# Pooled keys turned three at a time, scores of a head in two matmuls: pooled attention and a max-of-three feed-forward on one core

## The chip, the cores and the metric

The kernel runs on one core of a Trainium2 chip. The metric is the device time of one execution in microseconds (us), as the median of several runs. TensorE is the matrix engine (PE in the profile, PEld its weight loads), DVE is VectorE, ACT is ScalarE, POOL is GpSimd, SP the engine that issues many of the DMAs.

## The reference

Eight batches of attention with 8 heads, 576 positions and 64 elements per head. Keys and values are averaged over groups of 8 positions first, so each head has 576 queries and only 72 keys. The result, 4608 rows of 512, goes through a feed-forward layer whose hidden activation is the maximum of three products.

```
k_p = k.reshape(B, H, 72, 8, 64).mean(axis=3)
v_p = v.reshape(B, H, 72, 8, 64).mean(axis=3)
scores = scale * (q @ k_p.T);  attn = softmax(scores)
x = (attn @ v_p), heads side by side          # 4608 x 512
h = max(x @ w1, x @ w2, x @ w3)               # 4608 x 768
out = h @ w_out                               # 4608 x 512, float32
```

## The kernel before

The whole program is unrolled, and the order of instructions on each engine is the order in which the code issues them; a framework adds the semaphores. Tokens of the feed-forward are taken in nine blocks of 512. `block(n, plan, parts)` walks through the parts of block n (the hidden products at line 345, evacuated by ScalarE at line 351 and VectorE at line 353, and the output products at lines 390 and 394), and between two parts (a slot) it inserts the attention steps that `plan` names for that slot. Attention of batch n + 1 runs in this way between the matmuls of the feed-forward of block n. The last blocks (function `weave`) use the order written out in `ORDER`, with other products (lines 669 and 732).

The attention of a batch has these steps:

- GpSimd adds up groups of eight keys (`fold_k`, lines 150 to 153); for batch 1 VectorE does it, and batch 0 has a path of its own (`sum_k0`, `put_k0`). The sum `kp` has 96 partitions of 6 pooled keys each, 64 elements per key, in bfloat16.
- `k`: `turn_k` turns the keys so that the 64 elements lie on partitions. `keys` does it with six transposes on TensorE, one for each of the six keys of a partition, into one PSUM tile `pkt`. Two copies (`fill_kz`, line 193) take it to `kz`.
- `kz` holds the keys of all heads twice: once on partitions 0 to 63 with zeros below (parity 0) and once on partitions 64 to 127 with zeros above (parity 1). The reason is the layout of the queries: `qT` has nine groups of 64 queries per head, and two neighbouring groups lie above each other on the 128 partitions. A score matmul contracts over all 128 partitions and picks its half by the zeros. There are two `kz` buffers, for even and odd batches. For batches 1 and 2 both copies are on VectorE, for later ones parity 0 is copied by VectorE and parity 1 by ScalarE.
- `q`: the queries are turned by TensorE (`turn_q`) or, from batch 3, by a transposing DMA (`T`).
- `s0` to `s7`: `scores` of one head. Five groups of 64 queries belong to parity 0 and four to parity 1. They are written as 320 columns, then 192 and 64: the code splits where a PSUM bank ends, at column 512. Then `exp` on ScalarE, 72 partitions by 576.
- `v`, `x`: the weighted values, their division by the sum of the weights, and the turn of the result for the feed-forward.

In `plan`, for batches 3 to 5, `k` stands in slot 0 and the first scores in slot 2. For batch 2 (`plan1`) `k` is in slot 6 and the first score in slot 11; for batch 1 in slots 24 and 26 of block 0. Batch 6 is turned in slot 17 of block 4, batch 7 at the start of `ORDER` (scored flat, over 512 columns at a time). Batch 0 is scored by `scores4` and `scores2`.

In the middle of the program, the PSUM tag `att` holds two buffers of two banks (`pkt`, `psc`, `pav`), `pw` three of one bank, and `tr` one.

Of the kernel before, what the change touches and what calls it, by code (L numbers as in the profile page):

```python
# [14 lines left out]
def kernel(  # L15
# [11 lines left out]
    nc = tc.nc  # L27
    dt = mybir.dt
    F32, BF16, F16 = dt.float32, dt.bfloat16, dt.float16

    B, H, S, D = q.shape
    POOL = 8
    Sp = S // POOL
# [17 lines left out]
    const = ctx.enter_context(tc.tile_pool(name="const", bufs=1))  # L51
# [10 lines left out]
    def psum(shape, dtype, name, tag, bufs):  # L62
        return pools[-1].tile(shape, dtype, name=name, tag=tag, bufs=bufs)

    kts, vts, qbs, kps, qTs, ets = {}, {}, {}, {}, {}, {}
# [50 lines left out]
    ident = const.tile([128, 128], BF16, name="ident", tag="ident")  # L116
# [6 lines left out]
    for sign in (1, -1):  # L123
        nc.gpsimd.affine_select(
            out=pick, in_=pick, compare_op=ALU.is_ge, fill=0.0, base=7 * (sign < 0),
            pattern=[[sign, 6], [-8 * sign, 128]], channel_multiplier=6 * sign)
    for i in range(3):
        load_w(slice(256 * i, 256 * i + 256))
    nc.gpsimd.dma_start(
        out=wo_sb, in_=moe_w_out.rearrange("(jc p) c -> p jc c", p=128))  # L130
# [5 lines left out]
    load_v(2, nc.gpsimd)  # L136


    kz_all = [const.tile([128, 2, H, 128], BF16, name=f"kz{i}", tag=f"kz{i}")
              for i in range(2)]  # L140
    nc.vector.memset(kz_all[0], 0.0)
    vp_all = const.tile([Sp, B, H, 65], F16, name="vp", tag="vp")
    nc.vector.memset(vp_all[:, :, :, D:65], float(POOL))
    xT = const.tile([128, KCH, TOK], F16, name="xT", tag="xT")
# [13 lines left out]
    def fold_k(b, e, i0=0, i1=6):  # L158
        if b not in kps:
            new_kp(b)  # L160
        fold(e, kts[b][:, i0:i1], kps[b][:, i0:i1], F16 if e is nc.vector else F32)
# [12 lines left out]
    def turn_q(b, n0, n1, evac, tag):  # L174
        if b not in qTs:
            qTs[b] = sb2.tile([128, 2 * NG, 128], BF16, name="qT", tag="qT")
        pqt = psum([128, n1 - n0, 128], BF16, name="pqt", tag=tag[0],
                       bufs=tag[1])
        qf = qbs[b].rearrange("p hp t d -> p (hp t d)")
        for n in range(n0, n1):  # L180
            nc.tensor.transpose(pqt[:, n - n0, :], qf[:, 128 * n:128 * n + 128],
                                ident)
        evac(out=qTs[b][:, n0:n1, :], in_=pqt)  # L183

    def keys(b, tag):
        pkt = psum([D, 6, 96], BF16, name="pkt", tag=tag[0], bufs=tag[1])
        for i in range(6):
            nc.tensor.transpose(pkt[:, i, :], kps[b][:, i, :], ident[0:96, 0:96])  # L188
        return pkt

    def fill_kz(b, par, h0, h1, pkt, evac):
        rows = slice(64 * par, 64 * par + 64)
        evac(out=kz_all[b % 2][rows, par, h0:h1, 0:Sp].rearrange(
                 "p h (r i) -> p h r i", i=6),
             in_=pkt[:, :, 12 * h0:12 * h1].rearrange("p i (h r) -> p h r i", r=12))

    def turn_k(b):
        pkt = keys(b, ATT if len(pools) < 3 else SC)
        for par, evac in enumerate((nc.vector.tensor_copy, nc.scalar.copy)):
            fill_kz(b, par, 0, H, pkt, evac if b > 2 else nc.vector.tensor_copy)  # L200

    def score(b, h, out, tp, i0, i1):

        f = NG * (h // 2) + tp
        n = f // 2
        nc.tensor.matmul(out, kz_all[b % 2][:, f % 2, h, :],  # L206
                         qTs[b][:, n + i0:n + i1, 64 * (h % 2):64 * (h % 2) + 64],
                         start=True, stop=True)

    def exp(out, in_):  # L210
        nc.scalar.activation(out=out, in_=in_, func=FT.Exp, scale=1.0 / 64.0)  # L211

    def new_et(b):
        ets[b] = sb2.tile([Sp, H, S], F16, name="et", tag="et")

    def scores(b, h):
        psc = psum([128, 1024], F32, name="psc", tag="att", bufs=2)
        score(b, h, psc[:, 0:320], 0, 0, 5)
        score(b, h, psc[:, 320:512], 1, 0, 3)
        score(b, h, psc[:, 512:576], 1, 3, 4)  # L220
        exp(ets[b][:, h, :], psc[0:Sp, 0:S])

    def scores_flat(b, j):

# [11 lines left out]
    def turn_x(b, c0, keep, xn, tag, evac=nc.scalar.copy):  # L236
        if b > 2:
            g0 = S * b + c0
            nc.sync.dma_start_transpose(
                out=xT[:, :, g0 + keep:g0 + 128],  # L240
                in_=xn.rearrange("p g h d -> p (g h d)")[keep:128])
            return
        pxt = psum([128, KCH, 128], F16, name="pxt", tag=tag[0], bufs=tag[1])
        for kc in range(KCH):
            nc.tensor.transpose(  # L245
                pxt[:, kc, :],
                xn[:, kc // 2, 2 * (kc % 2):2 * (kc % 2) + 2, :], identh)
        g0 = S * b + c0
        evac(out=xT[:, :, g0 + keep:g0 + 128], in_=pxt[:, :, keep:128])  # L249

    def values(b, c0):
        tag = (ATT0, ATT, ("val", 1))[len(pools) - 1]
        pav = psum([128, 2, 512], F32, name="pav", tag=tag[0], bufs=tag[1])
        for h in range(H):
            nc.tensor.matmul(  # L255
                pav[:, h // 4, 65 * (h % 4):65 * (h % 4) + 65],
                ets[b][:, h, c0:c0 + 128], vp_all[:, b, h, :],
                start=True, stop=True)
        pv = pav[:, :, 0:260].rearrange("p g (h e) -> p g h e", e=65)
        rcp = sb3.tile([128, 2, 4], F32, name="rcp", tag="rcp")  # L260
        nc.vector.reciprocal(out=rcp, in_=pv[:, :, :, 64])  # L261
        xn = sb3.tile([128, 2, 4, D], F16, name="xn", tag="xn", bufs=6)
        nc.vector.tensor_tensor(  # L263
            out=xn, in0=pv[:, :, :, 0:D],
            in1=rcp.to_broadcast([128, 2, 4, D]), op=ALU.mult)
        return xn
# [11 lines left out]
    def do(b, steps):  # L278

        for name in steps.split():
            i = int(name[1:] or 0)
            if name[0] in "qQ":
                turn_q(b, *QS[i], nc.vector.tensor_copy if name[0] == "Q"
                       else nc.scalar.copy, TR)
            elif name[0] == "T":
                qTs[b] = sb2.tile([128, 2 * NG, 128], BF16, name="qT", tag="qT")
                nc.sync.dma_start_transpose(
                    out=qTs[b], in_=qbs[b].rearrange("p hp t d -> p (hp t d)"))  # L290
            elif name[0] == "k":
                turn_k(b)
            elif name[0] == "K":
                fold_k(b, nc.vector)
            elif name[0] == "s":
                if i == 0:
                    new_et(b)
                (scores if len(pools) < 3 else scores_flat)(b, i)
            elif name[0] == "d":
                sub_w(i)  # L300
            elif name[0] == "z":
                nc.vector.memset(kz_all[1], 0.0)
            elif name[0] == "w":
                turn_w(i, nc.scalar.copy if i % 2 else nc.vector.tensor_copy)
            elif name[0] == "v":
                xns[b, i] = values(b, CHUNKS[i][0])
            else:
                turn_x(b, *CHUNKS[i], xns[b, i], TR if b == 1 else ATT,
                       nc.vector.tensor_copy if name[0] == "X" else nc.scalar.copy)
# [4 lines left out]
    def sub_w(i, j0=0, j1=2, wi=(1, 2)):  # L314

        part = slice(256 * i + 128 * j0, 256 * i + 128 * j1)
        for t in [w_sb[w] for w in wi]:
            nc.vector.tensor_tensor(out=t[:, :, part], in0=t[:, :, part],  # L318
                                    in1=w_sb[0][:, :, part], op=ALU.subtract)

    def turn_w(jc, evac):
        pwt = psum([128, KCH, 128], F16, name="pwt", tag=TR[0], bufs=TR[1])
        for kc in range(KCH):
            nc.tensor.transpose(pwt[:, kc, :], w_sb[0][:, kc, bass.ts(jc, 128)], identh)
        evac(out=w1T[:, jc, :], in_=pwt.rearrange("p k c -> p (k c)"))
# [103 lines left out]

    def put_k0(a, par, evac):  # L430
        i = 3 * min(a, 1)
        evac(out=kz_all[0][64 * par:64 * par + 64, par, :, 0:Sp].rearrange(
                 "p h (r i) -> p h r i", i=6)[:, :, :, i:i + 3],
             in_=pk0[a].rearrange("p i (h r) -> p h r i", r=12))

# [23 lines left out]
    for par in range(2):  # L459
        put_k0(0, par, nc.scalar.copy)  # L460
# [36 lines left out]
    def block(n, plan, parts, folds=()):  # L497

        for slot, _ in enumerate(part for stage in parts for part in stage(n)):
            if slot == 0 and n > 0:  # L500
                pool_work(n, mms[-1])
            for b, steps in plan.get(slot, ()):
                if b < B:
                    do(b, steps)
            if folds and slot in FOLDS:
                next(folds.pop(0))
# [335 lines left out]
```

## Time and profile before

| | us |
|---|---|
| median of 5 runs (231.42 to 232.32) | 231.8 |
| the profiled execution | 231.8 |
| its span, first to last instruction | 230.1 |
| TensorE busy | 221.0 |
| GpSimd busy | 139.7 |
| VectorE busy | 128.6 |
| ScalarE busy | 121.1 |
| 42 transposes of keys, mean of one | 0.210 |
| 9 copies of keys on VectorE, mean of one | 0.749 |
| 5 copies of keys on ScalarE, mean of one | 0.630 |

The duration of a matmul in the profile includes its way through the array, so successive matmuls overlap: what a matmul costs the stream is the distance from its start to the next start. A group line has the line of the code, engine, operation, what is written and read, shapes and count, then the busy time in us and the mean of one in ns, then the idle time of the engine before it and what ended it. In a timeline the columns are start, length, engine, line, operation.

### The profile page before, as it was taken

To read this page: it belongs to the slowest core of one execution; us is meant where nothing else is said; L and a number is where in the kernel's file an instruction comes from. 1 tells how busy PE (TensorE), PEld (TensorE's weight loads), DVE (VectorE), ACT (ScalarE), POOL (GpSimd) and SP (SyncE) were. 2 spreads that over 40 slices of the span, in tenths; PEclk is the share of its full clock that TensorE was granted. 3 is DMA by queue.
4 is the path that set the end of the run, shared out by engine and by line. 5 is a ranking of instruction groups with operands and counts; after the bars stand their busy time and mean duration, and the time that the engine had idled before them with its cause. 6 is when DMAs were issued, how large, how long until landed. Compare 5 with 4: busy or idle time off the path is not lost.

```text
span 230.1 us, 4529 instructions
## 1 busy us (share of the span) xinstructions
PE 221.0 (96%) x1756; PEld 136.4 (59%) x1756; DVE 128.6 (56%) x235; ACT 121.1 (53%) x216; POOL 139.7 (61%) x115
## 2 busy tenths in 40 slices
PE   7788999999999999999999999999999999999991
PEld 2467645568655555545554555555777666786781
DVE  3668875048326333622462246279578877897720
ACT  2277425755864575247524852683786446464330
POOL 7974302999849999999999739900343433910010
PEclk9999999999999999999999999999999999999998
DMA  6999999999469999987998599961331535302336
GB/s 179 206 196 196 212 203 211 186 188 229 71 115 204 226 159 218 171 188 131 212 175 192 85 226 184 181 134 30 86 68 38 113 68 88 86 0 48 91 70 162
DMA packets 47157, 33.53 MB, mean 146 GB/s; under 512 B 27104, under 2 KB 41888, under 8 KB 47136
## 3 DMA queue, kind: packets, MB, share of 16 engines
q0 software_dynamic: 16944, 16.98, 45.8%
q1 hardware_dynamic: 30032, 16.13, 32.8%
q8 instruction: 14, 0.23, 0.4%
q10 hardware_dynamic: 160, 0.13, 0.3%
q14 instruction: 7, 0.06, 0.1%
HBM read 34.60 MB, written 9.44 MB: 191 GB/s over the span
## 4 chain that ended last, share of the span: by engine, by line
PE 89%; DMA 4%; DVE 2%; POOL 1%; issue 1%; ACT 1%; POOLq 0%; DVEq 0%
PE pw L345 27%; PE po L394 18%; PE po L390 12%; PE pA L732 7%; PE psc L206 5%; PE pav L255 4%; DMA vt<-in_v_dram 4%; PE pC L732 3%; PE pm L332 2%; PE oA L669 2%; PE pB L732 2%; PE pxt L245 1%; PE pkt L188 1%; DVE xn L263 1%; PE oC L669 1%
## 5 line engine op out<-in xcount | busy, mean ns | idle before, releaser
L345 PE MATMUL pw<-xT,mw 128*128 128x512 f16 (+1 forms) x336 | 73.1, 349 | 0.3 <-ACT xT L249 0.2
L394 PE MATMUL po<-mwo,hT 128*128 128x512 f16 (+1 forms) x198 | 46.8, 372 | 0.0
L353 DVE TENSOR_TENSOR hT<-t,pw 128x512 f16<-128x512 f16 (+1 forms) x42 | 25.5, 610 | 36.8 <-ACT et L211 25.1
L399 ACT COPY osb<-po 128x512 f32<-128x512 f32 (+1 forms) x32 | 18.5, 579 | 42.2 <-PE po L394 42.2
L345 PEld LDWEIGHTS <-mw 128*128 128x128 f16 x336 | 28.9, 98 | 19.7 <-DVE mw L318 0.6
L211 ACT ACTIVATE et<-psc 72x576 f16<-72x576 f32 (+2 forms) x54 | 35.2, 660 | 6.5 <-PE psc L206 6.3
L150 POOL TENSOR_TENSOR half<-vt 72x2048 f32<-72x2048 f16 x7 | 28.4, 4059 | 12.8 <-DMA vt<-in_v_dram 12.4
L390 PE MATMUL po<-wm,xT 128*128 128x512 f16 (+1 forms) x132 | 33.0, 373 | 0.0
L351 ACT ACTIVATE t<-pw 128x512 f16<-128x512 f32 (+1 forms) x42 | 22.5, 537 | 14.7 <-PE pw L345 13.0
L263 DVE TENSOR_TENSOR xn<-pav,rcp 128x512 f16<-128x512 f32 x40 | 27.7, 691 | 1.4
L394 PEld LDWEIGHTS <-hT 128*128 128x128 f16 x198 | 18.3, 97 | 16.2
L151 POOL TENSOR_TENSOR half<-half 72x1024 f32<-72x1024 f32 (+1 forms) x13 | 27.2, 2095 | 1.0
L206 PEld LDWEIGHTS <-kz 128*128 128x128 bf16 x191 | 17.6, 98 | 14.4 <-ACT qT L183 1.1
L206 PE MATMUL psc<-qT,kz 128*128 128x320 bf16 (+2 forms) x168 | 22.4, 246 | 0.8 <-DVE qT L183 0.6
L150 POOL TENSOR_TENSOR half<-ktFalse 96x1536 f32<-96x1536 f16 x6 | 18.6, 3095 | 5.3 <-DMA ktFalse<-in_k_dram 5.1
L255 PEld LDWEIGHTS <-et 72*128 72x128 f16 x320 | 15.4, 98 | 7.7 <-issue 0.4
L738 ACT CAST pad<-pA 128x512 f16<-128x512 f32 x27 | 15.3, 587 | 8.5 <-PE pA L732 6.0
L261 DVE RECIPROCAL rcp<-pav 128x8 f32<-128x8 f32 x40 | 8.2, 206 | 18.3 <-PE pav L255 18.1
L390 PEld LDWEIGHTS <-xT 128*128 128x128 f16 x132 | 11.9, 98 | 9.0
L255 PE MATMUL pav<-vp,et 72*128 72x65 f16 x320 | 16.9, 194 | 0.1
L713 DVE SCALAR_TENSOR_TENSOR hT<-pad 128x512 f16<-128x512 f16 x18 | 14.4, 810 | 1.8 <-ACT pad L742 1.4
L732 PEld LDWEIGHTS <-sw 128*128 128x128 f16 x144 | 13.7, 98 | 2.7
(106 smaller groups left out, 276.2 us busy)
## 6 DMA issues: line engine op xcount, KB each, us to landing
out_dram<-osb SPq DMA_DIRECT2D x62, 128.0 KB, 3.1
ktFalse<-in_k_dram POOLq DMA_DIRECT2D x7, 576.0 KB, 7.2
qb<-in_q_dram POOLq DMA_DIRECT2D x7, 576.0 KB, 13.5
vt<-in_v_dram POOLq DMA_DIRECT2D x7, 576.0 KB, 11.5
mw<-in_moe_w_dram POOLq DMA_DIRECT2D x9, 256.0 KB, 9.6
ktTrue<-in_k_dram SPq DMA_DIRECT2D x3, 384.0 KB, 5.2
mwo<-in_moe_w_out_dram POOLq DMA_DIRECT2D x1, 768.0 KB, 13.7
qb<-in_q_dram POOLq DMA_DIRECT2D x2, 288.0 KB, 7.9
```

Source lines behind the costliest of these rows:

```text
L150: e.tensor_tensor(out=f, in0=t[:, :, 0:4, :], in1=t[:, :, 4:8, :], op=ALU.add)
L151: e.tensor_tensor(out=f[:, :, 0:2, :], in0=f[:, :, 0:2, :], in1=f[:, :, 2:4, :], op=ALU.add)
L206: nc.tensor.matmul(out, kz_all[b % 2][:, f % 2, h, :], qTs[b][:, n + i0:n + i1, 64 * (h % 2):64 * (h % 2) + 64], start=True, stop=True)
L211: nc.scalar.activation(out=out, in_=in_, func=FT.Exp, scale=1.0 / 64.0)
L255: nc.tensor.matmul(pav[:, h // 4, 65 * (h % 4):65 * (h % 4) + 65], ets[b][:, h, c0:c0 + 128], vp_all[:, b, h, :], start=True, stop=True)
L263: nc.vector.tensor_tensor(out=xn, in0=pv[:, :, :, 0:D], in1=rcp.to_broadcast([128, 2, 4, D]), op=ALU.mult)
L345: mm = nc.tensor.matmul(pw, w_sb[wi][:, kc, bass.ts(jc, 128)], xT[:, kc, col], start=(kc == 0), stop=(kc == KCH - 1))
L351: nc.scalar.activation(out=t, in_=pw, func=FT.Relu)
L353: nc.vector.tensor_tensor(out=hT[:, jc, c0:c1], in0=t, in1=pw, op=ALU.max)
L390: nc.tensor.matmul(po, xT[:, kc, bass.ts(m, 128)], wm_sb[:, kc, c], start=(kc == 0), stop=False)
L394: nc.tensor.matmul(po, hT[:, jc, bass.ts(mm, 128)], wo_sb[:, jc, c], start=False, stop=(jc == JCH - 1))
L732: mm = nc.tensor.matmul(p[:, w], a[:, kc, bass.ts(g, 128)], b[:, kc, :], start=(i in FIRST and w + kc == 0), stop=(w + kc == 2), skip_grou ...
```

## The change

The keys of a batch are turned by three transposes in place of six. Each takes two of the six keys of a partition together, 128 columns, so that in `pkt` the even keys are on partitions 0 to 63 and the odd ones on 64 to 127. Each parity of `kz` is then filled by two copies, one for the even and one for the odd keys, each writing every second element of 72; four copies in all, on the same engines as before. `kz` becomes two tiles for each buffer, one per parity, and its two memsets become four of half the size. In `scores`, the 576 columns start at column 192 of the two banks, so that the border falls between the 320 columns of parity 0 and the 256 of parity 1, and two matmuls do.

```
-    kz_all = [const.tile([128, 2, H, 128], BF16, name=f"kz{i}", tag=f"kz{i}")
-              for i in range(2)]
-    nc.vector.memset(kz_all[0], 0.0)
+    kz_all = [[const.tile([128, H, 128], BF16, name=f"kz{i}{par}", tag=f"kz{i}{par}")
+               for par in range(2)] for i in range(2)]
+    for par in range(2):
+        nc.vector.memset(kz_all[0][par], 0.0)
...
     def keys(b, tag):
-        pkt = psum([D, 6, 96], BF16, name="pkt", tag=tag[0], bufs=tag[1])
-        for i in range(6):
-            nc.tensor.transpose(pkt[:, i, :], kps[b][:, i, :], ident[0:96, 0:96])
+        pkt = psum([128, 3, 96], BF16, name="pkt", tag=tag[0], bufs=tag[1])
+        for i in range(3):
+            nc.tensor.transpose(pkt[:, i, :],
+                                kps[b][:, 2 * i:2 * i + 2, :].rearrange("p i d -> p (i d)"),
+                                ident[0:96, 0:96])
         return pkt
-
-    def fill_kz(b, par, h0, h1, pkt, evac):
-        rows = slice(64 * par, 64 * par + 64)
-        evac(out=kz_all[b % 2][rows, par, h0:h1, 0:Sp].rearrange(
-                 "p h (r i) -> p h r i", i=6),
-             in_=pkt[:, :, 12 * h0:12 * h1].rearrange("p i (h r) -> p h r i", r=12))

     def turn_k(b):
         pkt = keys(b, ATT if len(pools) < 3 else SC)
         for par, evac in enumerate((nc.vector.tensor_copy, nc.scalar.copy)):
-            fill_kz(b, par, 0, H, pkt, evac if b > 2 else nc.vector.tensor_copy)
+            for odd in range(2):
+                (evac if b > 2 else nc.vector.tensor_copy)(
+                    out=kz_all[b % 2][par][64 * par:64 * par + 64, :, 0:Sp].rearrange(
+                         "p h (r i t) -> p h r i t", i=3, t=2)[:, :, :, :, odd],
+                     in_=pkt[64 * odd:64 * odd + 64].rearrange("p i (h r) -> p h r i", r=12))
...
-        nc.tensor.matmul(out, kz_all[b % 2][:, f % 2, h, :],
+        nc.tensor.matmul(out, kz_all[b % 2][f % 2][:, h, :],
...
     def scores(b, h):
         psc = psum([128, 1024], F32, name="psc", tag="att", bufs=2)
-        score(b, h, psc[:, 0:320], 0, 0, 5)
-        score(b, h, psc[:, 320:512], 1, 0, 3)
-        score(b, h, psc[:, 512:576], 1, 3, 4)
-        exp(ets[b][:, h, :], psc[0:Sp, 0:S])
+        score(b, h, psc[:, 192:512], 0, 0, 5)
+        score(b, h, psc[:, 512:768], 1, 0, 4)
+        exp(ets[b][:, h, :], psc[0:Sp, 192:768])
...
-                nc.vector.memset(kz_all[1], 0.0)
+                for par in range(2):
+                    nc.vector.memset(kz_all[1][par], 0.0)
...
-        evac(out=kz_all[0][64 * par:64 * par + 64, par, :, 0:Sp].rearrange(
+        evac(out=kz_all[0][par][64 * par:64 * par + 64, :, 0:Sp].rearrange(
```

## The prediction

> **What bounds the kernel now.** I read the page first (busy shares and the chain), then the timeline around one turn of the keys, then the groups by shape, then the tile view of `pkt`. On the page, TensorE is busy nearly all the time, the chain runs through it, and its clock is granted in full.
>
> ```profile
> PE 221.0 (96%) x1756; PEld 136.4 (59%) x1756; DVE 128.6 (56%) x235; ACT 121.1 (53%) x216; POOL 139.7 (61%) x115
> ...
> PEclk9999999999999999999999999999999999999998
> ...
> PE 89%; DMA 4%; DVE 2%; POOL 1%; issue 1%; ACT 1%; POOLq 0%; DVEq 0%
> ```
>
> From about 52 us to the end of its work at 225 us TensorE waits for almost nothing, so what its instruction stream sheds there comes off the time, unless a late copy puts a wait in its place. "Busy" hides small holes, so I look at start times. Timeline of TensorE alone, around the keys of batch 3 (start, length, operation):
>
> ```profile
> 78.44 0.38 PE L345 MATMUL pw<-xT,mw 128*128 128x512 f16 x1
> 78.75 0.44 PE L188 MATMUL pkt<-ident,kp 96*64 96x96 bf16 x6
> 79.12 0.39 PE L345 MATMUL pw<-xT,mw 128*128 128x512 f16 x1
> ```
>
> A 512-column matmul is followed by the next after 0.216 us in this trace (8 starts fill 1.73 us of the chain). Here 0.31 us pass before the first transpose: 0.096 of them are empty. Six transposes at 0.042 need 0.255; 0.375 pass. So a turn occupies 0.68 - 0.216 = 0.467 us, plus 0.011 by which the following matmul is late (0.227 instead of 0.216): 0.48. The same holes of 0.096 and 0.098 stand before and after each of the seven turns (37.1, 55.7, 78.7, 101.5, 124.3, 144.0, 159.5 us).
>
> **Part 1, three transposes with 128 weight columns.** The holes are found where the weights are 96x64. The value pooling has 96 rows and 128 columns:
>
> ```profile
> 13.37 0.81 PE L170 MATMUL pvp<-vt,pick 96*128 96x256 f16 x6
> 14.02 0.44 PE L206 MATMUL psc<-qT,kz 128*128 128x64 bf16 x4
> ```
>
> Six of 256 columns take 0.65 us to the next start, 0.109 each, the same as 256 columns elsewhere: no hole. I therefore cost the new turn (96x128) at 3 x 0.042 = 0.127 us and nothing around it. Saved: 0.48 - 0.127 = 0.355 us a turn, times 7 = 2.49 us. If 64 columns were not the cause and both holes stayed, only 3 x 0.042 = 0.127 a turn, 0.89 in all, would be saved.
>
> **Part 2, two score matmuls.** It drops one matmul in each of 8 heads of batches 1 to 6 (batch 7 is scored flat, batch 0 otherwise): 48. In the stream of starts near 105 us the three are 0.136, 0.083 and 0.028 apart; 256 columns elsewhere cost 0.109, so 0.111 becomes 0.109: 2 ns each, 0.1 us in all. The Trainium skill ("TensorEngine Tiling (Array Packing)", Instruction Overhead) gives every matmul about 60 cycles of overhead, which at this trace's 2.4 columns per ns would be 25 ns each, 1.2 us in all. The row decides: 64 columns at 28 ns are paid by columns, and the weight loads lie under the running matmul. Exp reads 576 columns over two banks as before: nothing.
>
> **Part 3, the copies.** Each 64x576 copy becomes two of 64x288 with every second element written. The nearest rows are batch 0's own 64x288 fills:
>
> ```profile
> L193 DVE COPY kz<-pkt 64x576 bf16<-64x576 bf16 x9 | 6.7, 749 | 12.5 <-PE pkt L188 12.4
> ...
> L193 ACT COPY kz<-pkt 64x576 bf16<-64x576 bf16 x5 | 3.2, 630 | 4.3 <-DVE kz L193 4.3
> ...
> L432 ACT CAST kz<-pk 64x288 bf16<-64x288 f32 x2 | 1.0, 476 | 4.1 <-PE pk L427 4.1
> ...
> L432 DVE CAST kz<-pk 64x288 bf16<-64x288 f32 x2 | 0.9, 473 | 0.7 <-PE pk L427 0.6
> ```
>
> They start 0.505 apart on both engines. Bounds: below, ACT's rows of 256 and 512 columns (372 and 585) put 288 at 398, and DVE's 749 for 576 at one column per 1.04 ns puts it at 449; above, no cheaper than before (749 and 630) if every second element costs like two. I take 473 and 476, as shape and type of the output agree.
>
> Times below are in the frame of the trace, as if nothing earlier had moved.
>
> *Batch 1 (all four on DVE).* The copies start at 37.36 (before 37.61, less the hole and three transposes, 0.25). The fourth ends at 37.36 + 3 x 0.505 + 0.473 = 39.35, and the second score matmul, which needs its weights, can start about 0.09 later (a weight load is 98 ns), 39.44. Before, it started at 39.44; unhindered it would now be there at 39.09. The 0.355 are lost, and nothing gives them back: the next hole, 0.29 at 46.2, is a wait for an exp that TensorE's own scores feed.
>
> *Batch 2 (four on DVE).* Queued behind them is the max of line 353:
>
> ```profile
> 56.15 1.51 DVE L193 COPY kz<-pkt 64x576 bf16<-64x576 bf16 x2 [0.54 <-PE pkt L188]
> 57.70 0.75 DVE L353 TENSOR_TENSOR hT<-t,pw 128x256 f16<-128x256 f16 x2
> ```
>
> It now starts at 55.905 + 4 x 0.505 = 57.93 instead of 57.70; it signals 0.43 after its start (57.70 to 58.13 before), so at 58.36, and the `pw` group that takes its buffer, at 58.44 before and 58.08 if unhindered, starts at 58.40: 0.04 of the 0.355 remains.
>
> *Batches 3 to 7 (two on DVE, two on ScalarE).* The tile view of `pkt` says what ScalarE's copy waits for:
>
> ```profile
> its engine sat idle before it (us, times) until:
>   PE pkt L188: 12.4, 6
>   DVE kz L193: 4.3, 5
> ```
>
> It waits for DVE's copy, though by their semaphores the first score weight loads wait for one of the two copies each (even parity for DVE, odd for ScalarE). So it isn't the tile `kz` that binds them but the read of one `pkt`, and splitting `kz` by parity takes no wait away. The Trainium skill ("PSUM — Partial Sum Buffer", PSUM bank collisions raise a hardware error) has the reason: two engines must not read one bank in the same 32 partitions at once, while other partitions of that bank are free. `pkt` is one bank, and the new copies read 64 partitions each. Kept by partitions, ScalarE's first copy waits for DVE's first, its second for DVE's second. Kept by whole banks, both wait for DVE's second. No row of the trace tells which; this is the largest unknown, so I work out both for batch 3.
>
> By partitions: DVE 78.98 to 79.45 and 79.48 to 79.96; ScalarE (free at 79.45) 79.49 to 79.96 and 79.99 to 80.47. The weight load for odd parity is now due at 80.86 - 0.355 = 80.51: in time. By banks: ScalarE 79.99 to 80.97, the score at about 81.07 where it was 80.995: the whole 0.355 is gone and 0.07 besides.
>
> Batch 6 has 1.5 us of slack (its keys are turned at 144.0, scored at 147.4): 0.355 in both. Batch 7: DVE is late there (copy at 160.60), so by partitions ScalarE ends at 162.09, `osb` behind it (162.28 before) frees its bank in time, 0.355 remains; by banks it ends at 162.6 and nothing remains.
>
> **Part 4, the split memsets** (lines 141 and 302, 0.91 us each): about 0.1 us more on DVE, while it waits for the first keys and at 30 us, where TensorE has no hole. Nothing.
>
> **The sum**, against the profiled execution (231.8 us, span 230.1, the rest of 1.7 unchanged; it equals the median of the runs). By partitions: batch 1 0, batch 2 0.04, batches 3 to 7 5 x 0.355 = 1.78, scores 0.1: 1.9, so **229.9 us**.
>
> **Rivals.** *A: whole banks.* 0 + 0.04 - 3 x 0.07 + 0.355 + 0 + 0.1 = 0.3 saved, 231.5; with copies at the lower bounds batches 3 to 5 give some 0.05 each and the sum is 0.8, 231.0. For it: a bank is the simplest unit to guard. Against it: nothing in this trace. *B (slower): the writes of every second element cost like full ones.* Copies of 750 (0.781 apart) and 630: batch 1's second score at 40.53 (1.09 late), batch 2's `pw` group at 59.51 (1.07 late), batches 3 to 5 0.27 late each, batch 7 0.22 late, batch 6 and the scores give 0.46 back: 2.7 us, 234.5. It decides once the copies exceed about 0.58 us, where 0.11 more per copy has eaten 1.9. Against it: batch 0's fills write runs of three and are only 23 (DVE) and 78 ns (ScalarE) over contiguous. *C: the holes stay.* Then the copies start 0.127 earlier, not 0.25; batch 1 ends 0.12 and batch 2 0.08 later than before, five turns give 0.127 each, the scores 0.1: 0.5 saved, 231.3. Against it: the 96x128 row.
>
> **How the numbers follow.** Main case 0.46 (own range 229.3 to 230.6, from copies at their lower bound to 40 ns longer), A 0.36, B 0.12, C 0.06. Range: 229.3 to 231.8 takes in A and C and leaves B and the ends out. This kernel's runs tell apart 0.3%, 0.7 us. Faster than that: nearly all of the main case and a third of A, 0.57. Within: most of A, C, 0.30. Slower: B and the tail of A, 0.13.
>
> **What would show it.** Right: `pkt` in 21 transposes of 96*128 with no hole around them, two score matmuls a head, ScalarE's first fill starting about 0.5 us after DVE's first. Wrong: ScalarE's first fill 1 us after it (A); fills above 0.58 us (B); 0.1 us before and after the new turn (C); or a wait of a `pw` or score matmul that I didn't foresee behind the longer DVE queue.

## The result and the profile after

The changed kernel takes 230.86 us (median of 29 runs, 230.47 to 232.13) beside 231.55 us for the kernel before (50 runs). The ratio is 0.9968, with a 95% interval of 0.9960 to 0.9976: faster by 0.3%, about 0.74 us. The forecast was 1.9 us. The time fell inside the range, but its size is not that of the main case, and the 0.3 us of rival A explain less than half of it.

The profiled execution took 230.47 us, its span 228.7. Its page, the lines that answer to those shown of before:

```profile
PE 219.3 (96%) x1687; PEld 134.6 (59%) x1687; DVE 129.6 (57%) x246; ACT 122.6 (54%) x221; POOL 140.5 (61%) x115
...
PEclk9999999999999999999999999999999999999998
...
PE 82%; DVE 6%; DMA 4%; ACT 3%; issue 2%; POOL 1%; DVEq 0%; ACTq 0%; POOLq 0%
```

TensorE has 69 matmuls less (21 transposes and 48 score matmuls) and is busy for 1.7 us less. But the chain now leaves it more often: DVE and ACT have 9% of it instead of 3%, and 4 of the 9 are the key copies (2% on each engine). The tile view of `pkt` (duration as least, median and most in ns, then first and last start in us):

```profile
L189 PE MATMUL pkt<-ident,kp x21: 203/204/208, 36.7 to 158.8; 96*128 96x96 bf16 x21
L198 DVE COPY kz<-pkt x18: 465/482/493, 37.0 to 160.4; 64x288 bf16<-64x288 bf16 x18
L198 ACT COPY kz<-pkt x10: 474/476/479, 79.5 to 161.4; 64x288 bf16<-64x288 bf16 x10
its engine sat idle before it (us, times) until:
  PE pkt L189: 11.0, 6
  DVE kz L198: 4.7, 5
```

The copies cost what was predicted (482 and 476 ns; 473 and 476 were taken). The last line is the one to read: ScalarE still sits idle in all five batches until VectorE is done, 4.7 us in all where it was 4.3. Timelines around the keys of batch 3, of before first (VectorE, ScalarE, and the scores on TensorE):

```profile
79.23 0.75 DVE L193 COPY kz<-pkt 64x576 bf16<-64x576 bf16 x1 [3.02 <-PE pkt L188]
80.01 0.63 ACT L193 COPY kz<-pkt 64x576 bf16<-64x576 bf16 x1 [0.56 <-DVE kz L193]
80.86 0.41 PE L206 MATMUL psc<-qT,kz 128*128 128x320 bf16 x3
```

There ScalarE was done at 80.64, 0.22 us ahead of the scores. After, VectorE and then ScalarE:

```profile
78.42 0.98 DVE L198 COPY kz<-pkt 64x288 bf16<-64x288 bf16 x2 [2.78 <-PE pkt L189]
```

```profile
79.48 0.96 ACT L198 COPY kz<-pkt 64x288 bf16<-64x288 bf16 x2 [0.60 <-DVE kz L198]
```

ScalarE starts 1.06 us after VectorE, when both of VectorE's copies are done, though its first copy and VectorE's second read different partitions. That is case A. TensorE pays for it one score later:

```profile
78.09 0.29 PE L189 MATMUL pkt<-ident,kp 96*128 96x96 bf16 x3
78.22 1.89 PE L346 MATMUL pw<-xT,mw 128*128 128x512 f16 x8
79.94 0.30 PE L207 MATMUL psc<-qT,kz 128*128 128x320 bf16 x1
80.50 0.28 PE L207 MATMUL psc<-qT,kz 128*128 128x256 bf16 x1 [0.26 <-ACT kz L198]
```

The turn is as short as predicted: three transposes from 78.09, the next matmul 0.13 us later, no hole on either side. The odd-parity score then starts 0.56 us after the even one. A matmul of 320 columns takes 0.136, so 0.42 us are empty. The same hole stands in batches 4 and 5 (0.43 in both), and in batch 7 one of 0.42 ahead of a projection at 162.56.

To see where on TensorE's stream the time is won and lost, I matched its matmuls, keys and scores left out, one by one with those of before. The table has by how many us a matmul starts later (+) or earlier (-) than in the profiled execution of before, near seven times of before's trace and at the last matmul; the second row is from a second profile of the changed kernel:

| near us | 30 | 50 | 70 | 95 | 118 | 141 | 152 | last |
|---|---|---|---|---|---|---|---|---|
| turns passed | none | batch 1 | 2 | 3 | 4 | 5 | 6 | 7 |
| after | -0.37 | -0.44 | -0.57 | -0.50 | -0.43 | -0.36 | -0.71 | -0.66 |
| after, second profile | -0.15 | -0.22 | -0.35 | -0.28 | -0.22 | -0.16 | -0.51 | -0.46 |

The first column is when the first values arrived, and it varies from one execution to the next. From there to the last matmul TensorE wins 0.29 us (0.31 in the second profile): almost only batch 6 pays. But the measured gain is 0.74. The rest lies behind the last matmul. From its start to the end of the span 5.10 us pass in before and 4.39 in after. The last stores on SyncE's queue, in before and then in after (start, time from the first issue to the end of the last):

```profile
222.43 3.83 SPq L648 DMA_DIRECT2D out_dram<-ob  x4
226.35 1.30 SPq L403 DMA_DIRECT2D out_dram<-osb  x2
```

```profile
221.77 2.88 SPq L649 DMA_DIRECT2D out_dram<-ob  x4
224.74 1.35 SPq L404 DMA_DIRECT2D out_dram<-osb  x2
```

The same four stores take 3.83 us to issue in before and 2.88 in after. One of them makes most of the difference: the second took 1.44 us there and 0.615 here. The queues of the two pages, before and then after, differ in the counts of two lines (packets, MB, share), both of queues that carry instructions:

```profile
q8 instruction: 14, 0.23, 0.4%
q14 instruction: 7, 0.06, 0.1%
```

```profile
q8 instruction: 13, 0.21, 0.4%
q14 instruction: 8, 0.07, 0.1%
```

On q14 it is a matter of counting: the eighth block of before starts at 231.1 us, just behind the end of the span. Each packet on q8 is a block of 16,384 bytes of code. By the trace's packet times the 14th of before is fetched at 223.1 us, when the slow store is being issued (from 223.12). After has one fetch less, its last at 216.9. That it is TensorE's code is inferred: of the engines' streams, TensorE's is the one that became shorter.

### The profile page after: what moved, and what is told of

Its sections match the earlier page's. It is cut to its first block, busy times and chain, and to the rows that moved or that the text cites. A ratio compares the mean times of both kernels' runs of the same rounds, so it can differ in the third digit from the quotient of the medians.

```text
span 228.7 us, 4412 instructions
## 1 busy us (share of the span) xinstructions
PE 219.3 (96%) x1687; PEld 134.6 (59%) x1687; DVE 129.6 (57%) x246; ACT 122.6 (54%) x221; POOL 140.5 (61%) x115
## 4 chain that ended last, share of the span: by engine, by line
PE 82%; DVE 6%; DMA 4%; ACT 3%; issue 2%; POOL 1%; DVEq 0%; ACTq 0%; POOLq 0%
PE pw L346 23%; PE po L395 18%; PE po L391 11%; PE pA L733 7%; PE psc L207 5%; PE pav L255 4%; DMA vt<-in_v_dram 4%; PE pC L733 3%; DVE kz L198 2%; PE pm L333 2%; PE oA L670 2%; PE pB L733 2%; DVE xn L263 2%; ACT kz L198 2%; PE pxt L245 1%
## 5 line engine op out<-in xcount | busy, mean ns | idle before, releaser
L346 PEld LDWEIGHTS <-mw 128*128 128x128 f16 x336 | 31.5, 98 | 21.5 <-DVE mw L319 0.6
L207 PE MATMUL psc<-qT,kz 128*128 128x320 bf16 (+2 forms) x120 | 22.9, 278 | 1.6 <-ACT kz L198 0.8
L207 PEld LDWEIGHTS <-kz 128*128 128x128 bf16 x143 | 13.1, 98 | 14.7 <-ACT kz L198 2.0
```

What stands on the lines that cost most here:

```text
L207: nc.tensor.matmul(out, kz_all[b % 2][f % 2][:, h, :], qTs[b][:, n + i0:n + i1, 64 * (h % 2):64 * (h % 2) + 64], start=True, stop=True)
L346: mm = nc.tensor.matmul(pw, w_sb[wi][:, kc, bass.ts(jc, 128)], xT[:, kc, col], start=(kc == 0), stop=(kc == KCH - 1))
```

## The experiments

Two questions: over which part of `pkt` the program keeps the reads of two engines apart (a bank, its partitions, the whole tile), and whether the end of the program is faster because of the change or by chance.

**The two kernels again.** No edit: a second profile of each.

> The changed kernel once more, for a second profile. Theory 1 (the turn of the keys wins 0.355 us seven times and the copies give most of it back): in the profile TensorE's part between its first value pooling and its last matmul is again only about 0.3 us shorter than before, with waits of about 0.4 us in batches 3, 4, 5 and 7 and 0.3 in batch 2; the time is 0.5 to 0.9 us under the kernel before, because start and end vary by several tenths from one execution to the next. Rival (a part of the gain lies at the start or at the end, by the split memsets or by earlier stores): the first value pooling again starts about 0.4 us earlier than the 13.37 us of before, or the tail after the last matmul is again about 0.7 us shorter than the 4.8 us of before.

> The kernel before once more, for a second profile. If the tail hangs on the fourteenth fetch of code: again fourteen fetches, the last about 2 us before the last matmul, and a tail of 5.1 us. If the tail of 5.1 us was chance: somewhere between 4.3 and 5.1 without the long store.

The changed kernel: 230.82 us, ratio 0.9968 (0.9956 to 0.9981); waits as in the first trace, tail 4.39 us to the hundredth. The kernel before: 231.46 us, again 14 fetches, the last at 223.0, the second store 1.305 us to issue, tail 4.70. The start (the first column of the table) isn't systematic: between -0.41 and +0.20 us in the seven traces that have the change's memsets and no other edit of the start. The end is.

**The scores alone.** The kernel before, with only the edit of `scores`:

```
-        score(b, h, psc[:, 0:320], 0, 0, 5)
-        score(b, h, psc[:, 320:512], 1, 0, 3)
-        score(b, h, psc[:, 512:576], 1, 3, 4)
-        exp(ets[b][:, h, :], psc[0:Sp, 0:S])
+        score(b, h, psc[:, 192:512], 0, 0, 5)
+        score(b, h, psc[:, 512:768], 1, 0, 4)
+        exp(ets[b][:, h, :], psc[0:Sp, 192:768])
```

> Only the two score matmuls with the shift of 192 columns; keys, copies and memsets as before. By the trace (a dropped matmul of 64 columns gives back 2 ns, 48 times): 0.1 us, ratio 0.9996. By the rule of about 60 cycles of overhead per matmul: 1.2 us, ratio 0.995.

(The rule of 60 cycles is the one that the prediction takes from the Trainium skill, "TensorEngine Tiling (Array Packing)", Instruction Overhead.)

230.90 us, ratio 0.9970 (0.9958 to 0.9981). On TensorE's stream it wins 0.11 us, 2 ns for each of 48 matmuls, as the row of starts had said. Yet the time falls by 0.7 us, as much as with the whole change: the tail is 4.40 us, with 13 fetches. So nearly all that the change brings comes with this small part, and not by the matmuls' own time.

**Two readers of other partitions.** The changed kernel, with VectorE copying the even keys (partitions 0 to 63 of `pkt`) and ScalarE the odd ones (64 to 127):

```
-        for par, evac in enumerate((nc.vector.tensor_copy, nc.scalar.copy)):
-            for odd in range(2):
+        for odd, evac in enumerate((nc.vector.tensor_copy, nc.scalar.copy)):
+            for par in range(2):
```

> The changed kernel with the four copies dealt out by the half of pkt that they read: VectorE copies the even keys (partitions 0 to 63) for both parities, ScalarE the odd keys (64 to 127), so that the two engines never read the same partitions of the bank. If reads of one bank are kept apart by partitions: ScalarE's first copy starts together with VectorE's first, no score of batches 3 to 5 and 7 waits, 1.7 us under the changed kernel: about 229.3, ratio to before 0.990. If by whole banks: ScalarE's first copy still starts about 1.07 us after VectorE's first, and the time is that of the changed kernel within 0.3 us, ratio 0.997.

230.64 us, ratio 0.9967 (0.9954 to 0.9979). ScalarE still starts 1.06 us after VectorE (at 78.61), although the two never read the same partition:

```profile
79.67 0.99 ACT L198 COPY kz<-pkt 64x288 bf16<-64x288 bf16 x2 [0.59 <-DVE kz L198]
```

By itself this run leaves a doubt, as both engines now also write into one `kz` tile. The next two don't.

**Two banks, one tile or two.** The transposes are made twice, and each engine reads its own copy. For batches 3 to 6 the two copies are the two banks of one tile, for batch 7 two tiles:

```
...
+        elif tag is SC:
+            pkts = [keys(b, tag), keys(b, tag)]
+        else:
+            both = psum([128, 2, 1024], BF16, name="pkt2", tag=tag[0], bufs=tag[1])
+            pkts = [keys(b, tag, both[:, par, 0:288].rearrange("p (i c) -> p i c", i=3))
+                    for par in range(2)]
...
-                     in_=pkt[64 * odd:64 * odd + 64].rearrange("p i (h r) -> p h r i", r=12))
+                     in_=pkts[par][64 * odd:64 * odd + 64].rearrange("p i (h r) -> p h r i", r=12))
```

> The changed kernel, but for batches 3 to 7 the three wide transposes are made twice, into two PSUM banks; VectorE copies from the one, ScalarE from the other. If ScalarE's wait in the changed kernel comes from the shared bank of pkt: its first copy now starts beside VectorE's first, the waits of about 0.42 us of the scores of batches 3 to 5 and of batch 7's line 391 are gone, 0.127 us per turn are paid for the second set; against the changed kernel 4 x 0.42 - 5 x 0.127 = 1.0 us less, about 229.8, ratio to before 0.992. If the wait has another source (the tiles of the keys, the semaphores): the waits stay and the time is 0.6 us over the changed kernel, 231.4.

231.01 us, ratio 0.9972 (0.9958 to 0.9986). ScalarE in batch 3 and in batch 7:

```profile
79.56 0.97 ACT L207 COPY kz<-pkt 64x288 bf16<-64x288 bf16 x2 [0.73 <-DVE kz L207]
...
159.63 0.97 ACT L207 COPY kz<-pkt 64x288 bf16<-64x288 bf16 x2 [0.52 <-PE pkt L190]
```

With two banks of one tile it waits for VectorE (which started at 78.50, so 1.06 us again). With two tiles it waits for TensorE alone and starts 0.71 us ahead of VectorE (160.34). The unit is the tile.

**Two tiles in every batch from 3 on.**

```
-        pkt = keys(b, ATT if len(pools) < 3 else SC)
+        tag = ATT if len(pools) < 3 else SC
+        if b < 3:
+            pkts = [keys(b, tag)] * 2
+        elif tag is SC:
+            pkts = [keys(b, tag), keys(b, tag)]
+        else:
+            pkts = [keys(b, tag), keys(b, TR)]
...
-                     in_=pkt[64 * odd:64 * odd + 64].rearrange("p i (h r) -> p h r i", r=12))
+                     in_=pkts[par][64 * odd:64 * odd + 64].rearrange("p i (h r) -> p h r i", r=12))
```

> The changed kernel, but from batch 3 on the three wide transposes are made twice, into two PSUM tiles of their own: VectorE reads one, ScalarE the other, so that no tile has two readers. It costs 0.127 us more of TensorE per turn, five turns, 0.64 us. Theory that the guard covers a whole PSUM tile: ScalarE's first copy starts beside VectorE's first instead of 1.06 us later, the waits of 0.42 to 0.43 us ahead of the odd scores in batches 3 to 5 and of 0.42 in batch 7 are gone (1.7 us), and the time is about 1.0 us below the changed kernel, near 229.8, ratio 0.991 to 0.993. Rival, that ScalarE is late for another reason (its own queue, or the order in which both engines write the key tile): the waits of batches 3 to 5 stay, and the time is 231.0 to 231.5.

230.56 us, ratio 0.9954 (0.9933 to 0.9975). ScalarE and then TensorE in batch 3:

```profile
79.19 0.97 ACT L204 COPY kz<-pkt 64x288 bf16<-64x288 bf16 x2
```

```profile
78.36 0.42 PE L189 MATMUL pkt<-ident,kp 96*128 96x96 bf16 x6
78.62 1.89 PE L352 MATMUL pw<-xT,mw 128*128 128x512 f16 x8
80.35 0.41 PE L213 MATMUL psc<-qT,kz 128*128 128x320 bf16 x2
```

ScalarE starts 0.49 us after VectorE (78.70), and only because its own activation ran until 79.16. The two scores follow each other, and all four holes of 0.42 to 0.43 us are gone. TensorE wins 1.35 us to its last matmul, 1.06 more than in the changed kernel, as expected (1.70 of holes less 0.64 for 15 more transposes). The time does not follow: it is 0.7 us above the 229.8 expected, because the tail is 5.28 us. There the stores are issued as fast as in the changed kernel, but the last one takes 3.06 us from its issue to landing instead of 2.19: of the 16 signals of its landing 15 are there by 227.04 us, and one comes at 227.86. On the other code queue a block of 8,192 bytes is fetched at 226.4 us, in the middle of it; no other trace has such a fetch between the last issue and the end. There is this one trace of it, so the cause of this 0.87 us stays open.

**Fetches of code moved by padding.** In the first of three, the 17 warm-up matmuls at the start were cut into five each:

```
-            nc.tensor.matmul(wm, warm[:, 0:128], warm, start=True, stop=True)
+            for c0, c1 in ((0, 104), (104, 206), (206, 308), (308, 410), (410, 512)):
+                nc.tensor.matmul(wm[:, c0:c1], warm[:, 0:128], warm[:, c0:c1],
+                                 start=True, stop=True)
```

> The changed kernel with each of its 17 warm-up matmuls cut into five narrower ones of the same 512 columns in all: 68 matmuls and 68 weight loads more at a time when TensorE waits for inputs, 3512 instructions on TensorE where the changed kernel has 3376 and the kernel before 3514. Theory (the tail of before is longer because TensorE's fourteenth block of code is fetched while the last results are stored, and the change needs only thirteen): a fourteenth fetch about 2 us before the last matmul, one store on SP taking about 1.4 us to issue instead of 0.6, tail 5.0 instead of 4.4 us, and 0.6 to 0.7 us over the changed kernel: 231.4. Rival (the tail is shorter for another reason): tail 4.4, 230.8.

232.50 us, ratio 1.003 (1.0015 to 1.0044). The 14th fetch is back at 223.2, the store beside it takes 1.216 us, the tail is 4.64. But the time rose by twice what the theory says: all later matmuls start 0.9 us later relative to the changed kernel's trace, since the start itself was slowed. (The profiled execution took 231.54 us, near the fastest of the 22; what the slower ones lost, the trace can't show.) The place of the padding spoiled the run, so I moved it into the middle: matmuls of the hidden layer are cut into two halves, first 72 of them, then 128.

```
-            for kc in range(KCH):
-                mm = nc.tensor.matmul(pw, w_sb[wi][:, kc, bass.ts(jc, 128)],
-                                      xT[:, kc, col],
+            cuts = (0, 256, 512) if n == 2 or (n == 3 and jc < 3) else (0, c1 - c0)
+            for s0, s1 in zip(cuts, cuts[1:]):
+                for kc in range(KCH):
+                    mm = nc.tensor.matmul(pw[:, s0:s1], w_sb[wi][:, kc, bass.ts(jc, 128)],
+                                          xT[:, kc, col.start + s0:col.start + s1],
...
```

(128: `n in (2, 3) or (n == 4 and jc < 4)`.)

> The changed kernel, with 72 of the hidden layer's matmuls of 512 columns (block 2, and half of block 3) cut into two of 256: the same work, 144 more rows of matmuls and weight loads on TensorE, 3,520 in all, about as many as the kernel before has (3,514). The cuts lie in the middle of the kernel, far from its start and its end. Theory that a fetch of code at the end costs the time: the 14th block of code is fetched again, near 223 us and amid the last stores, the second of the last four stores of SyncE takes 1.2 to 1.4 us to issue instead of 0.62, the tail behind the last matmul is 4.6 to 5.1 us instead of 4.39, and the time is 0.2 us (the cuts, 3 ns each) and 0.3 to 0.6 us above the changed kernel: 231.3 to 231.6. Rival, that the tail belongs to the changed keys and scores: the tail stays at 4.4 us, and the time near 231.0.

> As with 72 cuts, but with 128 matmuls cut (blocks 2 and 3, and part of block 4): 3,632 rows. The 14th fetch of code then comes some 6 us earlier, near 216 to 217 us, before the last four stores of SyncE. Theory that it is the meeting in time that costs, not the number of fetches: no store of the last four takes over 0.7 us to issue, the tail is 4.4 us with 14 fetches, and the time is 0.3 to 0.4 us above the changed kernel for the cuts alone, 231.0 to 231.3. Rival, that 14 fetches cost as such: the tail is 4.6 to 5.1 us here too, and the time 231.5 to 231.8.

With 72 cuts: 231.85 us, ratio 1.0003 (0.9990 to 1.0015). With 128 cuts, so with more work: 231.07 us, ratio 0.9971 (0.9961 to 0.9981). SyncE's last stores, with 72 cuts and then with 128:

```profile
223.59 3.88 SPq L651 DMA_DIRECT2D out_dram<-ob  x4
227.56 1.42 SPq L406 DMA_DIRECT2D out_dram<-osb  x2
```

```profile
222.61 2.92 SPq L651 DMA_DIRECT2D out_dram<-ob  x4
225.62 1.30 SPq L406 DMA_DIRECT2D out_dram<-osb  x2
```

Both have 14 fetches. With 72 cuts the last comes at 224.2 us, the second store of the four starts at 224.29 and takes 1.62 us, and the tail is 5.27. With 128 cuts the last fetch comes at 217.5 us, the second store takes 0.62 and the tail is 4.40; the fourth store takes 0.86, over the 0.7 that was expected, but it takes 0.83 in the changed kernel too. It is the meeting in time that costs, not the number of fetches. The time with 72 cuts is 0.25 us above the band expected; why isn't known. Its profiled execution was the slowest of its 14 runs (233.12 us), and the trace has a wait of 1.17 us at the start of a block (147.6 us, for tokens that a DMA turns), which I hadn't foreseen; that wait is about what sets this execution apart from the median. The comparison of the tails stands without it, as a tail is counted from the last matmul.

Thirteen traces in one table, all but that of one failed run told below (fetches on queue q8; tail: from the start of the last matmul to the end of the span; second store: its start and the time its issue took):

| kernel | fetches, last at us | second store at us, us | tail us |
|---|---|---|---|
| before, two profiles | 14, 223.1 and 223.0 | 223.12, 1.44 and 223.19, 1.31 | 5.10, 4.70 |
| 72 cuts | 14, 224.2 | 224.29, 1.62 | 5.27 |
| warm-up padded | 14, 223.2 | 223.33, 1.22 | 4.64 |
| six wide transposes (below) | 14, 222.4 | 222.66, 1.29 | 4.81 |
| 128 cuts | 14, 217.5 | 223.31, 0.62 | 4.40 |
| after, two profiles | 13, 216.9 and 217.7 | 222.47 and 222.67, 0.62 both | 4.39 both |
| scores alone | 13, 213.4 | 223.02, 0.62 | 4.40 |
| other partitions | 13, 216.1 | 222.68, 0.62 | 4.36 |
| two banks | 13, 213.1 | 222.65, 0.62 | 4.36 |
| six wide, fixed tiles (below) | 13, 212.5 | 222.22, 0.62 | 4.49 |
| two tiles | 13, 211.8 | 221.71, 0.62 | 5.28 |

In five traces a fetch begins at most 0.3 us ahead of the second store, and in those five alone it is slow. The rest of the same traces agrees, though not without exception. SyncE issues 884 stores of the result in them, and 34 take over 1 us; 28 of these overlap a fetch on q8, though only 91 of the 884 do. Of 29 stores that begin within 0.3 us behind the start of such a fetch, 21 take over 1 us and eight take 0.47. So a meeting is mostly slow, not always, and six slow stores met no fetch on q8. That the fetched code is TensorE's is now shown as well: cuts on TensorE alone added the fetch and then moved it.

**Six wide transposes, two copies.** If 128 weight columns are what closes the holes, one can have that and keep the copies of before: each transpose takes key i and, for padding, key i + 1 along, and rows 64 to 127 of `pkt` are never read. The sixth takes a seventh slot that has to be cleared, and to make room the operand of the warm-up matmuls is 448 columns instead of 512. The scores stay in three matmuls.

```
-        kps[b] = sb2.tile([96, 6, D], BF16, name="kp", tag="kp")
+        kps[b] = sb2.tile([96, 7, D], BF16, name="kp", tag="kp")
+        (nc.vector if b == 1 else nc.gpsimd).memset(kps[b][:, 6, :], 0.0)
...
-            nc.tensor.transpose(pkt[:, i, :], kps[b][:, i, :], ident[0:96, 0:96])
+            nc.tensor.transpose(pkt[:, i, :], kps[b][:, i:i + 2, :].rearrange("p i d -> p (i d)"),
+                                ident[0:96, 0:96])
```

> Only the holes around the turn are taken away: six transposes as before, but each with 96x128 weights (key i and its neighbour; only the first 64 output partitions are used), two copies as before, three score matmuls. It needs a seventh key slot, cleared once per batch on GpSimd or VectorE, and 64 columns less in the warm-up operand. Theory 1 (weights of 64 columns make the holes of 0.096 and 0.098): 0.225 us per turn, 1.6 us in all, since the copies start 0.1 earlier and stay inside their slack: 230.0, ratio 0.993. Rival (the holes come from something else at the turn): no change, 231.5.

231.26 us (229.78 to 234.69), ratio 0.9976 (0.9960 to 0.9992). Each turn wins 0.22 us as expected. But at the starts of two blocks TensorE now waits for tokens that a DMA turns, 0.35 us at 100.2 and 0.79 at 146.3. From 46 us on GpSimd's loads are issued 0.5 to 1.4 us later than in the first trace of before, and the new clears are an obvious suspect. But in the second trace of before, which has no clears and no such wait, they are 0.7 to 1.4 us later too, and the tokens of the block at 146 us land at 146.34 there and at 146.20 here: TensorE comes earlier, rather than the tokens later. So the clears aren't shown to be the cause. And the fetch meets the stores. A first try at clearing only once, with two fixed key tiles and two score matmuls:

> Six wide transposes and two copies, as in the run with six wide transposes, with the two score matmuls of the change; the seventh key slot lies in two fixed tiles that VectorE clears once at the start, so GpSimd's queue is that of before (the warm-up operand is again 64 columns narrower). Theory (holes only from weights of 64 columns, the copies in their slack, and the variation of the run with six wide transposes from GpSimd's clears, which made its loads late): 7 x 0.22 + 0.1 on TensorE and 0.7 at the end, 2.3 us, about 229.3, ratio 0.990, and no wait at line 346 of 0.3 us or more at the start of a block. Rival (wide transposes cost elsewhere): the waits at the start of blocks return, ratio 0.995 to 0.998 with a wide spread.

It took 292.56 us, ratio 1.262. The sums of keys run two batches ahead here, so that with two fixed tiles the sum of batch b + 2 comes ahead of the turn of batch b: TensorE waited for later batches' sums and turned their keys. It says nothing about the transposes. With three fixed tiles, the slot cleared once by VectorE at the start (the six wide transposes and two copies as above, and two score matmuls; the warm-up operand has its 512 columns again and shares its memory with `wm_sb`, which is made later):

```
+    kp_all = [const.tile([96, 7, D], BF16, name=f"kp{i}", tag=f"kp{i}") for i in range(3)]
+    for kp in kp_all:
+        nc.vector.memset(kp[:, 6, :], 0.0)
...
-        kps[b] = sb2.tile([96, 6, D], BF16, name="kp", tag="kp")
+        kps[b] = kp_all[b % 3]
```

> Six transposes of 96x128 per batch instead of twelve of 96x64 (a head's 96 keys of the two pooled groups and padding in one transpose each), copied whole in two copies as before the change, with the scores of a head in two matmuls. The seventh key slot that the last wide transpose reads is cleared once at the start on VectorE, in three fixed tiles, so GpSimd's queue carries nothing new. Theory: the drains of 0.19 us at each turn go and nothing else moves: 7 turns by about 0.22 us and 0.1 us of dropped score matmuls on TensorE's stretch, and a tail without the late fetch of code (13 fetches), 0.4 us: 2.0 to 2.3 us, 229.3 to 229.7, ratio about 0.991, and no wait of 0.3 us or more at the start of a block. Rival, that the block-start waits of the earlier version with six wide transposes came of the shorter turns themselves: they return, ratio 0.995 to 0.998.

(The kernel before has six transposes a batch, not twelve, and what are called drains are the holes of 0.096 and 0.098 us; what the array does in them no trace shows.)

230.17 us (229.72 to 230.99), ratio 0.9943 (0.9921 to 0.9964): the lowest median of all, 0.7 us below the changed kernel, though the intervals of the two against the kernel before overlap a little. The tile view of `pkt`:

```profile
L191 PE MATMUL pkt<-ident,kp x42: 203/206/217, 37.2 to 159.0; 96*128 96x96 bf16 x42
L198 DVE COPY kz<-pkt x9: 744/750/752, 37.7 to 159.9; 64x576 bf16<-64x576 bf16 x9
L198 ACT COPY kz<-pkt x5: 630/630/631, 79.9 to 160.7; 64x576 bf16<-64x576 bf16 x5
```

Copies of 750 and 630 ns as before the change, and no score waits for them: with VectorE done after one copy of 0.75 us instead of two, ScalarE starts 0.8 us behind it instead of 1.06 and needs 0.63 instead of 0.96. TensorE wins 1.07 us to its last matmul where 1.6 were expected. Three waits take the rest: 0.28 ahead of the turn of batch 2, which now waits for the key sum on GpSimd, and 0.12 and 0.19 at the starts of two blocks. No wait of 0.3 us or more is left at the start of a block. But that doesn't convict the clears of the first version: with 72 cuts, where GpSimd's work is untouched, there is one of 1.17. When a block's tokens land differs between executions by more than these waits (at 144.9 and 146.3 us in the two traces of before), so a shorter stream can run into it; what sets that time I didn't test.

## Why the prediction was right or wrong

**What bounds the kernel: right for the middle, incomplete at the end.** TensorE's stream sets the time from 52 us on. But "what its instruction stream sheds there comes off the time" takes the 5.1 us behind the last matmul as unchanged, without a reason, and this step failed: the tail is shorter by 0.71 us against the profiled execution of before, by 0.31 against its second profile. (The "rest of 1.7", which lies outside the span, did stay: 230.47 less 228.7.) With the 0.29 to 0.31 of TensorE's stretch this covers the 0.74 measured. A fetch of TensorE's code met a store on SyncE's queue; the change took 138 matmuls and weight loads out, and the fetch went. The two runs with cuts show that it is the meeting that costs.

**Part 1: right.** The holes of 0.096 and 0.098 us are gone, the turn costs 0.130 where 0.127 was said, and each turn taken by itself wins 0.35. Rival C is out, and the six wide transposes show that the width of the weights makes the holes.

**Part 2: right.** 0.11 us for the 48 matmuls, measured alone, where the row gave 0.1 and the rule of the Trainium skill ("TensorEngine Tiling (Array Packing)", Instruction Overhead) would give 1.2, taken as a cost on top of the columns. (The section also says that a matmul of one column takes as long as one of 60; read as such a floor, it agrees with 64 columns at 28 ns.) That the time fell by 0.7 us all the same would have looked like the rule's truth without the trace.

**Part 3, the copies: right in price, wrong in the choice.** The price of a copy was within 2%, which leaves rival B out. Batches 1 and 2 kept 0.07 and 0.13 us where 0 and 0.04 were said. In batch 2 a hole of before at 58.9 us, 0.06, went too. In batch 1 the loss comes only in part from the copies: the second score waits 0.15 us for VectorE, and 0.16 us go before that, at 37.4, where TensorE waits to turn more queries until just after ScalarE has copied the first of them (36.86 to 37.55). Before, that copy was over 0.23 us ahead of it; this wait was not in the prediction.

The step that failed is "Kept by partitions, ScalarE's first copy waits for DVE's first": it waits for VectorE's second. Batches 3 to 5 lose the whole 0.355 and 0.07 more each, batch 6 keeps it, and batch 7 loses it and 0.07 more. That is the account of rival A, 0.3 us, for batches 3 to 6. That the total fits to 0.01 us is in part luck: batches 1 and 2 gave about 0.1 us more than A had for them, and batches 3 to 7, by the table with the scores' gain in it, about 0.1 less.

And A's reason was wrong as well: the unit is neither the bank nor the partitions but the tile, as two banks of one tile wait and two tiles don't. I had inferred the granularity of a semaphore from a rule about hardware (in the Trainium skill, "PSUM — Partial Sum Buffer", PSUM bank collisions raise a hardware error). The rule says what two engines may not do together, and advises guards by bank and 32 partitions; the wait is set by the program's own bookkeeping, and that is coarser. What the hardware would do without the wait, no run here shows. In before, the line "DVE kz L193: 4.3, 5" stood for a wait on a tile as well as for one on its partitions: nothing in that trace could decide, and the choice of 0.46 against 0.36 rested on the rule alone.

**Part 4: right.** No hole near the memsets.

## What to carry to other kernels

Where two engines are to read one PSUM result side by side, give each a tile of its own: here a second set of three transposes (0.127 us) buys back a wait of 0.42 to 0.43 on TensorE, though a longer tail took most of that back in its one trace. A stage made shorter pays only as far as everything that feeds the next stage keeps pace, so follow the consumers, batch by batch, before multiplying a saving by a count. And look at the last microseconds of both traces before crediting a small gain to the edit: a change in the number of instructions can move a fetch of code onto, or off, the last stores.

## What I had not expected of the hardware

The meeting of a fetch and a store: a block of 16,384 bytes of TensorE's code, fetched when SyncE issues a store of the result, goes with an issue of 1.2 to 1.6 us for that store instead of 0.62, and the stores behind it come later. The end of the program moves from 4.4 or 4.5 us behind the last matmul to 4.6 to 5.3. A fetch of 8,192 bytes on the other code queue, at 223.2 us with 128 cuts, just ahead of the second store there, did no such thing (0.62 us). And the price of going from 128 weight columns to 64 and back, 0.19 us a turn, falls away if the 64 are merely padded to 128: six wide transposes cost the stream 0.21 to 0.22 us a turn less than six narrow ones.
